# Weights decoded with their sign in the high word's Prelu, and a table that gives every operation its place

## The chip, the cores and the metric

The kernel runs on one core of a Trainium2 chip. Its engines are named as the profile names them: PE is TensorE (PE for its matmuls, PEld for its weight loads), DVE is VectorE, ACT is ScalarE, POOL is GpSimd, SP is SyncE, which issues the DMAs. The metric is the device time of one execution in microseconds (us), the median of the runs shown; lower is better.

## What is computed

The reference, cut to what matters: attention over 16 heads of 768 positions in which a key counts only if its 6-bit hash bucket is the query's, then two feed-forward blocks on 1536 tokens of 512 features.

```python
q_bits = (np.einsum('bhsd,dk->bhsk', q, proj) > 0).astype(np.int64)   # k_bits likewise
mask = q_bucket[:, :, :, None] == k_bucket[:, :, None, :]
scores = np.where(mask, scale * np.matmul(q, k.transpose(0, 1, 3, 2)), -1000000000.0)
attn = np.exp(scores - np.max(scores, axis=-1, keepdims=True))
x = np.matmul(attn / (np.sum(attn, axis=-1, keepdims=True) + 1e-09), v)
...
h = x @ w_in                                   # 512 -> 2048
x = (h * (1.0 / (1.0 + np.exp(-h)))) @ w_out   # 2048 -> 512
a, b = x @ w1, x @ w2                          # 512 -> 1024 each
out = ((a * b) @ w3) @ w_out2                  # 1024 -> 1024 -> 512
```

The weights of the feed-forward blocks reach the chip as 64-bit floating-point numbers.

## The kernel before

**Stages.** The 16 heads go by as 8 pairs of heads (n = 0 to 7), each as 12 units of 128 queries (two heads, six units each). A unit is: `scores` on PE (four matmuls into one of two score tiles), `peak` on DVE (the row maximum, L733), `exp` on ACT (L739, into one of two tiles P), `swap` on DVE (a transpose in blocks of 32, L757). When the 12 units of a pair are swapped, `weigh` on PE multiplies by V (six calls of 32 matmul statements of 32-row tiles; the profile counts two instructions for each, 64 a call), ending in four accumulators: both tiles `acc` and both tiles `turn`. `move` takes them to X, and `norm` divides by the row sums, which have gone through memory and back (`flip`, `unload`, `invert`, `send`, `spread`). Before its units, a pair needs its q and k in two parts each: `halve` (ACT or POOL), `left` (POOL, tiles qa and kb) and copies by DMA, after which `qraw` and `kraw` take the next pair's.

**Feed-forward.** w3 and the second w_out are multiplied together while attention runs (`product`, 192 matmuls of 128x512). The first block's first cells (`rise`, then `fall`, on the first 512 tokens, whose heads are done early) run there too; all other cells follow the last `weigh`. There PE has nothing but matmuls of 128x512. The tokens 512 to 1535 are multiplied in seven products of sums and differences in place of eight; their inputs (tiles y0 and y1, 14 each) are made by ACT and DVE out of X after the last pair's `norm`.

**Decoding.** All weights come in 36 pieces of two halves, 72 halves of 128x512 numbers. For each half a DMA brings 64-bit words to a tile `raw`. `high` (ACT) scales the high words into the exponent range of 32 bits, `low` (ACT or POOL) makes the top bits of the low words, `join` (DVE, L380) shifts the one and ORs the other. The sign was lost in the shift. For the 28 halves that are needed before attention ends, `high` writes to a PSUM tile (`acc`, under a token `joint`), `side` (ACT, L391) takes the sign of the high words into x, and `signed` (POOL, L394) multiplies; `raw` is given back after `side`. For the 44 others `high` writes to SBUF, and `sign` (DVE, L385) ANDs the sign bit out of `raw` and ORs it in. Then `hi` and `lo` make the two parts of a tile `piece` (lines 324, 327 and 320).

**What sets the order.** Every step is an `op` with a due time, its dependencies, the engines that it may run on with a cost in ns, and the buffers that it takes and gives. `Plan.run` plays all engines forward with these costs, picks for each engine the operation with the smallest due time among those that could start next, and emits instructions in that order; each engine then runs its own in that fixed order, with semaphores for what it needs. The due time is a formula at the place of the call, to which `shift` adds an offset from the table `OFF`, by the step's name and one of five stages. An op marked `port` is planned so that DVE and POOL don't run at the same time.

## Time and profile before

| | us |
|---|---|
| median of 3 runs (lowest to highest) | 722.84 (722.47 to 724.21) |
| span of the profiled execution | 720.6 |
| PE busy in it | 680.8 |
| DVE busy | 548.8 |
| ACT busy | 395.8 |
| POOL busy | 276.7 |

The span is from the first to the last instruction of the profiled execution; the median of the runs is 2.2 us more, which lies around the span. In the profile times are from the span's start. The last transpose of attention ends at 279.5, the last `weigh` about 293; what follows is feed-forward alone. So the question for each engine is how busy it is before 279.5, and how busy after 293. In a row of the timeline the idle time ahead of an instruction and what ended it stand in square brackets. In a row of the groups of instructions stand the count, the busy time in us, the mean of one in ns, and then the idle time ahead of them.

### The profile page before, as it was taken

What the parts mean: (1) busy time and instruction counts of PE and PEld (TensorE: products, weight loads), DVE (VectorE), ACT (ScalarE), POOL (GpSimd) and SP (SyncE); (2) the same over time, 40 slices, a digit from 0 to 9 for tenths busy, and PEclk for the clock granted to TensorE, in tenths of its full rate; (3) what the DMA queues carried; (4) which work ended last, traced back from release to release, by engine and by line L of the source; (5) the groups of instructions that cost most, each with busy time, mean ns of one, the idle gap of its engine ahead of it and who ended that gap; (6) DMA issues with size and microseconds to landing.
All of it is one profiled execution on the core that took longest, in us unless ns stands there. A gap on an engine that the chain in (4) does not pass through costs nothing.

```text
span 720.6 us, 14384 instructions
## 1 busy us (share of the span) xinstructions
PE 680.8 (94%) x5792; PEld 549.1 (76%) x5792; DVE 548.8 (76%) x799; ACT 395.8 (55%) x717; POOL 276.7 (38%) x265
## 2 busy tenths in 40 slices
PE   8697999999998999799999999999999999999997
PEld 5565777766776777688888888888888888888876
DVE  6799886958594988898889987967897637738155
ACT  5868676858585656656564453452546635323030
POOL 3967696866876711433203213022213230220000
PEclk9887899979999999999999999999999999999999
DMA  8535465655555342302212303020102220200004
GB/s 240 174 129 142 122 161 163 152 162 137 175 154 175 84 142 79 105 22 96 73 45 88 123 25 102 23 80 15 45 29 63 85 73 1 101 30 1 0 1 175
DMA packets 22883, 68.34 MB, mean 95 GB/s; under 512 B 3873, under 2 KB 4641, under 8 KB 22305
## 3 DMA queue, kind: packets, MB, share of 16 engines
q1 hardware_dynamic: 22816, 67.43, 31.0%
q8 instruction: 45, 0.74, 0.4%
q14 instruction: 22, 0.17, 0.1%
HBM read 55.58 MB, written 5.29 MB: 84 GB/s over the span
## 4 chain that ended last, share of the span: by engine, by line
PE 73%; DVE 9%; ACT 5%; issue 4%; DMA 4%; POOL 3%; SPq 0%; DVEq 0%; ACTq 0%; POOLq 0%
PE more L1181 18%; PE more L1019 14%; PE more L1137 8%; PE acc L775 7%; PE acc L1181 7%; PE score L717 5%; PE acc L1019 5%; PE turn L775 3%; PE acc L1137 2%; DVE pt L757 2%; ACT P L739 2%; PE acc L857 2%; DVE st L733 2%; DVE y L327 2%; DMA kraw<-in_kT 1%
## 5 line engine op out<-in xcount | busy, mean ns | idle before, releaser
L1019 PE MATMUL more<-y,piece 128*128 128x512 f32 x474 | 117.6, 389 | 0.7 <-ACT qraw L320 0.7
L733 DVE TENSOR_REDUCE st<-score 128x1 f32<-128x770 f32 x96 | 89.0, 941 | 33.8 <-PE score L717 31.2
L1019 PEld LDWEIGHTS more<-y,piece 128*128 128x128 f32 x474 | 88.9, 188 | 19.6 <-ACT qraw L320 1.2
L739 ACT ACTIVATE P<-score,st 128x768 f32<-128x768 f32 x96 | 85.8, 895 | 28.7 <-DVE st L733 18.4
L757 DVE STREAM_TRANSPOSE pt<-P 128x768 f32<-128x768 f32 x96 | 90.5, 958 | 5.8 <-ACT P L739 5.7
L1181 PE MATMUL more<-gh,piece 128*128 128x512 f32 x268 | 91.7, 390 | 0.1
L775 PE MATMUL turn<-pt,V 32*64 32x193 f32 x1536 | 78.4, 344 | 8.9 <-issue 8.8
L775 PE MATMUL acc<-pt,V 32*64 32x193 f32 x1536 | 77.9, 344 | 1.4 <-issue 0.8
L1200 DVE SCALAR_TENSOR_TENSOR X<-more,X 128x512 f32<-128x512 f32 x88 | 59.5, 685 | 23.7 <-PE more L1181 23.0
L775 PEld LDWEIGHTS acc<-pt,V 32*64 32x64 f32 x1536 | 60.5, 139 | 10.8 <-issue 7.5
L775 PEld LDWEIGHTS turn<-pt,V 32*64 32x64 f32 x1536 | 58.0, 138 | 12.0 <-issue 11.7
L717 PE MATMUL score<-ka,qa 128*128 128x384 f32 x168 | 51.7, 390 | 12.7 <-ACT P L739 11.3
L1137 PE MATMUL more<-x,piece 128*128 128x512 f32 x264 | 62.9, 389 | 0.0
L1181 PEld LDWEIGHTS more<-gh,piece 128*128 128x128 f32 x268 | 50.3, 188 | 10.9 <-DVE X L1200 0.5
L1137 PEld LDWEIGHTS more<-x,piece 128*128 128x128 f32 x264 | 49.6, 188 | 10.3
L717 PEld LDWEIGHTS score<-ka,qa 128*128 128x128 f32 x168 | 28.7, 201 | 33.4 <-ACT P L739 23.8
L1181 PE MATMUL more<-gl,piece 128*128 128x512 f32 x134 | 52.2, 389 | 0.0
L857 PE MATMUL acc<-piece,piece 128*128 128x512 f32 x192 | 50.3, 397 | 1.4 <-ACT X L794 1.4
L374 POOL TENSOR_SCALAR t<-raw 128x512 uint32<-128x512 uint32 x15 | 10.8, 717 | 100.9 <-DVE x L385 28.9
L370 ACT ACTIVATE t<-raw 128x512 uint32<-128x512 uint32 x46 | 30.8, 670 | 32.9 <-DMA raw<-in_w 21.1
L717 PE MATMUL score<-kb,qb 76*128 76x384 f32 x168 | 46.2, 357 | 0.6 <-DMA kb<-bits 0.6
L1181 PE MATMUL more<-piece,gh 128*128 128x512 f32 x144 | 44.3, 389 | 0.0
(195 smaller groups left out, 1450.2 us busy)
## 6 DMA issues: line engine op xcount, KB each, us to landing
raw<-in_w SPq DMA_DIRECT2D x28, 512.0 KB
raw<-in_wo SPq DMA_DIRECT2D x21, 512.0 KB
V<-in_v SPq DMA_DIRECT2D x16, 384.0 KB
raw<-in_win SPq DMA_DIRECT2D x12, 512.0 KB
qraw<-in_qT SPq DMA_DIRECT2D x8, 384.0 KB
kraw<-in_kT SPq DMA_DIRECT2D x8, 384.0 KB
invb<-inverse SPq DMA_DIRECT2D x16, 192.0 KB
out<-X SPq DMA_DIRECT2D x12, 256.0 KB
```

Of the source, the lines that this page charges most:

```text
L327: engine[e].tensor_tensor(out=dst, in0=src, in1=hi.bitcast(F32), op=ALU.subtract)
L370: nc.scalar.activation(out=plan[t], in_=pair(raw)[:, :, 0], func=AF.Copy, scale=0.875 * 2.0 ** -29, bias=0.49)
L717: nc.tensor.matmul(out=sc[:, g, :HF], lhsT=lhs[:k, qs], rhs=rhs[:k, g * HF:g * HF + HF], start=(k == 128), stop=(k != 128),)
L733: nc.vector.tensor_reduce(out=plan[uk("st")][:, 0:1], in_=plan[uk("S")][:, :, :HF + 1], op=ALU.max, axis=AX.XY, negate=True)
L739: nc.scalar.activation(out=plan[uk("P")], in_=plan[uk("S")][:, :, :HF], func=AF.Exp, bias=s[:, 0:1], accum_out=plan[key("sums")][:, par * ...
L757: nc.vector.transpose(plan[mine][:, :, 32 * i:32 * i + 32], plan[uk("P")].rearrange("p g (b i) -> p (g b) i", i=32))
L775: nc.tensor.matmul(out=to[a][64 * side:64 * side + 64, :GW + 1], lhsT=V[rows_, c, side], rhs=plan[key(f"pt{side}")][rows_, c, :GW + 1], st ...
L857: nc.tensor.matmul(out=plan[key + ("ps",)], lhsT=w[:, a, k], rhs=r[:, c], start=(k == 0 and n == 0), stop=(k == 7 and n == 2),)
L1019: nc.tensor.matmul(out=plan[bk[b]], lhsT=w[:, a], rhs=y, start=(opens and j == 0 and m == 0), stop=(j == 1 and m == 2), skip_group_check=True)
L1137: nc.tensor.matmul(out=plan[key], lhsT=w[:, a], rhs=x, start=(k == 0 and n == 0), stop=(k == 3 and n == 2))
L1181: nc.tensor.matmul(out=plan[key], lhsT=a, rhs=x, start=(f == 0 and n == 0), stop=(f == 1 and n == 2))
L1200: nc.vector.scalar_tensor_tensor(out=dst, in0=plan[key], scalar=by, in1=dst, op0=ALU.mult, op1=ALU.add)
```

## The change

**The sign.** `high` becomes Prelu, the activation that multiplies negative inputs by a slope: scale 2^-112 as before, slope -(2^32). A negative high word comes out positive with an exponent larger by 32, and the shift by 3 carries that bit into the sign bit. So `sign` (44 on DVE), `side` (28 on ACT) and `signed` (28 on POOL) are gone. All halves now go one way: `low`, then `high`, both into SBUF tiles of one pool of four x tiles (two x and two t before); `raw` is given back after both; `join` works in place. PSUM, the token `joint` and the split into early and late halves are out of it.

**The order.** `OFF`, the stages and the due times are replaced by `PLACE`: one number for each of the some 2950 operations, in the order of their creation, and the smaller goes first. Some costs of the plan are changed, and a switch of PE between `weigh` and other matmuls is given a cost of 110. Which steps exist and what each computes is otherwise the same; some buffers are given back after a few more dependencies than before. Where an engine could be chosen, a few operations change theirs.

```diff
-STAGES = (60, 210, 285, 445)
-OFF = {
...
-def shift(name, due):
-    return OFF[name][sum(due >= x for x in STAGES)] if name in OFF else 0.0
+PLACE = [
+    220, 21, 22, 23, 19, 24, 28, 29, 90, 101, 53, 93, 91, 248, 325, 328, 326, 46, 48, 50, 43, 124, 128, 210, 199, 223,
...
-PE_FREE, PE_COL, PE_TURN, PE_MORE = 13.5, 1 / 2.4, 110.0, 16.0
+PE_FREE, PE_COL, PE_TURN, PE_SWITCH = 13.5, 1 / 2.4, 110.0, 110.0
...
-        due += shift(kind or emit.__qualname__.split(".")[-1], due)
-        o = Op(on, emit, deps, due * 1000.0, take, give, size)
-        o.port = port
+        o = Op(on, emit, deps, PLACE[len(self.ops)], take, give, size)
+        o.port, o.tiled = port, tiled
...
+            if e == "PE" and o.tiled != tiled:
+                ns, tiled = ns + PE_SWITCH, o.tiled
...
-    plan.buffers("joint", [None])
...
-    plan.buffers("x", tiles(wp, "x", [128, STEP], F32, 2))
-    plan.buffers("t", tiles(wp, "t", [128, STEP], U32, 2))
+    plan.buffers("x", tiles(wp, "x", [128, STEP], F32, 4))
...
-                def high(e, raw=raw, w=w):
-                    nc.scalar.activation(out=plan[w], in_=pair(raw)[:, :, 1].bitcast(F32), func=AF.Copy, scale=2.0 ** -112)
+                def high(e, raw=raw, x=x):
+                    nc.scalar.activation(out=plan[x], in_=pair(raw)[:, :, 1].bitcast(F32), func=AF.Prelu,
+                                         scale=2.0 ** -112, alpha=-(2.0 ** 32))
...
-                def sign(e, raw=raw, x=x, m=m):
-                    engine[e].scalar_tensor_tensor(
-                        out=u32(x), in0=pair(raw)[:, :, 1], scalar=0x80000000, in1=u32(m),
-                        op0=ALU.bitwise_and, op1=ALU.bitwise_or,
-                    )
-
-                def side(e, raw=raw, x=x):
-                    nc.scalar.activation(out=plan[x], in_=pair(raw)[:, :, 1].bitcast(F32), func=AF.Sign)
-
-                def signed(e, x=x, t=t):
-                    nc.gpsimd.tensor_tensor(out=plan[x], in0=plan[t].bitcast(F32), in1=plan[x], op=ALU.mult)
-
-                a = op({"ACT": 570}, high, [load], due, [("joint", key), ("x", x), ("W", w)] if beside else [("x", x)])
-                b = op({"ACT": 570, "POOL": 590}, low, [load], due, [("t", t)])
-                j = op({"DVE": 608}, join, [a, b], due + 1, give=[w, key] if by_pool else [t] if beside else [], port=not beside)
...
+                b = op({"ACT": 570, "POOL": 590}, low, [load], due, [("x", x), ("x", t)])
+                a = op({"ACT": 570}, high, [b], due)
+                op({"": 0}, lambda e: None, [a, b], due, give=[raw])
+                j = op({"DVE": 608}, join, [a, b], due + 1, give=[t], port=True)
```

**How the order moves.** In these rows names ending in 77 and 78 are the tiles `turn`, 79 and 80 the score tiles, 81 and 82 the tiles `acc`, 83 to 89 the pieces.

PE, in the `weigh` of the fifth pair (n = 4): before, the first run of 96 `weigh` statements ends, one unit is scored, and the next run of 64 begins.

```order
L775 MATMUL turn_77<-pt_125,V_105 64x193
L717 MATMUL score_79<-ka_114,qa_110 128x384 x2
L717 MATMUL score_79<-kb_116,qb_112 128x384 x2
L775 MATMUL acc_82<-pt_127,V_105 64x193
L775 MATMUL acc_82<-pt_125,V_105 64x193
```

Now, at the same place of the same pair:

```order
L836 MATMUL turn_77<-pt_125,V_105 64x193
L777 MATMUL score_80<-ka_114,qa_110 128x384 x2
L777 MATMUL score_80<-kb_116,qb_111 128x384 x2
L777 MATMUL score_79<-ka_114,qa_110 128x384 x2
L777 MATMUL score_79<-kb_116,qb_111 128x384 x2
L836 MATMUL acc_81<-pt_127,V_105 64x193
```

Two units stand between the runs in place of one. In the fourth pair the runs were 96, 64 and 32 statements with one unit between, and are 32, 64, 64 and 32 with two; in the fifth 96, 64, 32 with one, and now with two; in the sixth 32, 64, 96 with one, and now 96, 64, 32 with two.

POOL, while the sixth pair's q and k are prepared (qa and kb by `left`, L327 before and L407 now; L394 is `signed`). Before:

```order
L327 TENSOR_TENSOR piece_88<-x_93,piece_88 128x512
L327 TENSOR_TENSOR piece_89<-x_92,piece_89 128x512
L327 TENSOR_TENSOR kb_115<-kraw_104,ka_113 64x768
L833 TENSOR_TENSOR X<-X,invb_128 128x768
L394 TENSOR_TENSOR x_93<-t_95,x_93 128x512
L324 TENSOR_SCALAR ka_114<-kraw_104 64x768
L324 TENSOR_SCALAR piece_89<-x_93 128x512
L327 TENSOR_TENSOR kb_116<-kraw_104,ka_114 64x768
L327 TENSOR_TENSOR piece_89<-x_93,piece_89 128x512
L394 TENSOR_TENSOR x_92<-t_94,x_92 128x512
L327 TENSOR_TENSOR qa_110<-qraw_103,qa_110 64x768
```

Now:

```order
L407 TENSOR_TENSOR kb_116<-kraw_104,ka_114 64x768
L407 TENSOR_TENSOR qa_110<-qraw_103,qa_110 64x768
L407 TENSOR_TENSOR piece_87<-x_93,piece_87 128x512
L451 TENSOR_SCALAR x_93<-raw_91 128x512
L894 TENSOR_TENSOR X<-X,invb_128 128x768
L681 TENSOR_SCALAR bits_108<-bits_108,sel 128x384
L407 TENSOR_TENSOR x_97<-X,x_97 128x512
L404 TENSOR_SCALAR qa_109<-qraw_103 64x768
L407 TENSOR_TENSOR kb_115<-kraw_104,ka_113 64x768
L407 TENSOR_TENSOR qa_109<-qraw_103,qa_109 64x768
```

The sign multiplications among the `left` steps (qa and kb) are gone. The steps of one head stand next to each other, the other head's after the `norm`.

PE, right behind the last `weigh`. Before, 24 matmuls of `fall` and 24 of `rise` on the first 512 tokens (x_97) come ahead of the first matmul on the others (y):

```order
L1181 MATMUL acc_81<-piece_85,piece_84 128x512 x6
L1181 MATMUL more_3493<-piece_85,piece_84 128x512 x6
L1181 MATMUL more_3494<-piece_85,piece_84 128x512 x6
L1181 MATMUL more_3495<-piece_85,piece_84 128x512 x6
L1137 MATMUL more_3496<-x_97,piece_86 128x512 x12
L1137 MATMUL more_3497<-x_97,piece_86 128x512 x12
L1137 MATMUL more_3498<-y_0_3442,piece_89 128x512
```

Now 18 come ahead of it; the 24 of `rise` stand before the last `weigh`:

```order
L1245 MATMUL acc_82<-piece_84,piece_83 128x512 x3
L1245 MATMUL acc_81<-piece_84,piece_83 128x512 x3
L1245 MATMUL acc_82<-piece_84,piece_83 128x512 x3
L1245 MATMUL more_3477<-piece_84,piece_83 128x512 x3
L1245 MATMUL more_3478<-piece_84,piece_83 128x512 x6
L1201 MATMUL more_3479<-y_0_3426,piece_88 128x512
```

Before the last `weigh` begins to run, PE has 72 matmuls of feed-forward cells behind it in the old order and 96 in the new one.

## Rows read from the trace of the kernel before

**Rows 1.** Busy time by stretch: stretch, length, each engine, granted clock, DMA.

```profile
0.00:279.50 279.50, 248.75 (x3556) 192.29 (x3556) 219.97 (x287) 195.57 (x366) 186.21 (x165) 0.93 0.53 150
293.00:720.60 427.60, 422.61 (x1854) 348.80 (x1854) 319.46 (x499) 195.40 (x343) 89.06 (x98) 1.00 0.17 57
```

**Rows 2.** The chain that ended last, in order of time: feed-forward matmuls.

```profile
587.96 14.96 PE more L1019 x66
```

**Rows 3.** Waits of DVE in 150:166, 186:200, 217:234 (total, times, longest).

```profile
DVE st L733 <- PE score L717: 8.7, 3, 5.6
...
DVE st L733 <- PE score L717: 6.9, 2, 3.7
...
DVE st L733 <- PE score L717: 5.4, 2, 5.2
DVE fv L322 <- PE turn L775: 4.5, 1, 4.5
```

**Rows 4.** Busy time by stretch, as rows 1: two of these stretches.

```profile
150.00:166.00 16.00, 15.28 (x400) 12.44 (x401) 6.69 (x10) 5.81 (x12) 7.99 (x9) 0.79 0.33 103
186.00:200.00 14.00, 12.89 (x403) 10.55 (x402) 6.16 (x10) 5.04 (x12) 10.58 (x10) 1.00 0.47 133
```

**Rows 5.** The same chain in attention: two loads and a sign step.

```profile
63.93 4.61 DMA raw<-in_w
...
95.77 3.16 DMA raw<-in_w
...
136.04 1.30 POOL x L394
```

**Rows 6.** Groups of instructions: the two DVE steps of a unit.

```profile
L757 DVE STREAM_TRANSPOSE pt<-P 128x768 f32<-128x768 f32 x96 | 90.5, 958 | 5.8 <-ACT P L739 5.7
L733 DVE TENSOR_REDUCE st<-score 128x1 f32<-128x770 f32 x96 | 89.0, 941 | 33.8 <-PE score L717 31.2 <-PE score L729 2.1
```

**Rows 7.** Timeline of PE: two units of `scores`, then `weigh`.

```profile
55.36 0.62 PE L717 MATMUL score<-ka,qa 128*128 128x384 f32 x2
...
56.97 0.39 PE L775 MATMUL acc<-pt,V 32*64 32x193 f32 x4
```

**Rows 8.** Groups of instructions: sign steps, `high`, the table load.

```profile
L394 POOL TENSOR_TENSOR x<-t,x 128x512 f32<-128x512 f32 x28 | 35.8, 1281 | 9.7 <-ACT x L391 8.1 <-POOL qa L327 1.1 <-DVE t L380 0.2
L391 ACT ACTIVATE x<-raw 128x512 f32<-128x512 f32 x28 | 18.6, 666 | 0.1
L366 ACT ACTIVATE acc<-raw 128x512 f32<-128x512 f32 x28 | 17.7, 631 | 5.0 <-PE acc L526 2.4 <-DVE t L380 2.3
L366 ACT ACTIVATE x<-raw 128x512 f32<-128x512 f32 x23 | 15.2, 668 | 7.6 <-DVE piece L327 2.6 <-DMA raw<-in_win 1.9 <-DMA raw<-in_wo 1.9
L320 ACT ACT_TABLE_LOAD x1 | 1.3, 1283 | 0.7 <-PEq L1278 0.7
```

**Rows 9.** `join`, one line's instructions (min/median/max ns): a PSUM operand, then none.

```profile
L380 DVE SCALAR_TENSOR_TENSOR t<-acc,t x28: 650/677/692, 12.3 to 235.0; 128x512 uint32<-128x512 uint32 x28
L380 DVE SCALAR_TENSOR_TENSOR t<-x,t x32: 635/684/1161, 253.2 to 636.9; 128x512 uint32<-128x512 uint32 x32
```

**Rows 10.** Groups of instructions: DVE steps that read two SBUF tiles.

```profile
L327 DVE TENSOR_TENSOR piece<-x,piece 128x512 fp32r<-128x512 f32 x38 | 28.4, 752 | 4.7 <-ACT piece L320 3.9 <-POOL piece L324 0.4
L327 DVE TENSOR_TENSOR x<-X,x 128x512 fp32r<-128x512 f32 x1 | 1.4, 1448 | 0.0
```

**Rows 11.** Groups of instructions: the eviction that frees a PSUM bank.

```profile
L1200 DVE SCALAR_TENSOR_TENSOR X<-more,X 128x512 f32<-128x512 f32 x88 | 59.5, 685 | 23.7 <-PE more L1181 23.0
```

**Rows 12.** Timeline of PE from the end of the last `weigh`.

```profile
293.42 2.93 PE L1181 MATMUL acc<-piece,piece 128*128 128x512 f32 x6 [0.45 <-ACT X L794]
...
305.87 2.88 PE L1137 MATMUL more<-y,piece 128*128 128x512 f32 x12
```

**Rows 13.** Timeline of DVE in the same stretch.

```profile
296.38 0.69 DVE L1200 SCALAR_TENSOR_TENSOR X<-acc,X 128x512 f32<-128x512 f32 x1 [1.40 <-PE acc L1181]
296.99 3.63 DVE L327 TENSOR_TENSOR y<-X,y 128x512 fp32r<-128x512 f32 x5
```

More of the change, by code (lines that the diff above doesn't have):

```diff
@@ L187, in run @@
         wire = port = 0.0
+        tiled = False
         for o in self.ops:
@@ L370, in low @@
                         nc.scalar.activation(
-                            out=plan[t], in_=pair(raw)[:, :, 0], func=AF.Copy, scale=0.875 * 2.0 ** -29, bias=0.49
+                            out=u32(t), in_=pair(raw)[:, :, 0], func=AF.Copy, scale=0.875 * 2.0 ** -29, bias=0.49
                         )
@@ L418, in piece @@
             soon, behind = need < BEGIN + SOON, need >= T_END - 20
-            h = op({"POOL": pool1(STEP), "ACT": act(STEP)} if soon or behind else {"POOL": pool1(STEP)}, hi, [j, opener], due + 3, take=first)
+            h = op({"POOL": pool1(STEP), "ACT": act_sbuf(STEP)} if soon or behind else {"POOL": pool1(STEP)}, hi, [j, opener], due + 3, take=first)
             opener = h
@@ L1097, in lsh_attention_moe_kernel @@
         users = [[], []]
+        before_that = lastly[-3:-2] if cell not in early else []
         for f in range(1 if part == 1 else 2):
@@ L1223, in lsh_attention_moe_kernel @@
         fallen.setdefault((part, c), []).extend(falls)
+        if cell not in early:
+            lastly.append(mine[bk][-1])
+        for f, last in enumerate(users):
+            risen.setdefault((part, c, f), []).extend(last)
         if kind == PAIR:
@@ L1228, in lsh_attention_moe_kernel @@
             op({"": 0}, lambda e: None, fallen[part, c], due, give=[name])
-            for of, last in zip(ofs, users):
-                op({"": 0}, lambda e: None, last, due, give=[of[0]])
+            for f, of in enumerate(ofs):
+                op({"": 0}, lambda e: None, risen[part, c, f], due, give=[of[0]])
     plan.total = plan.run()
```

144 lines of the change are left out of this document (37 added, 107 removed), and 145 rows, old and new, of the table PLACE.

## Prediction

> **What bounds the kernel now.** I read the busy time by stretch first, because a mean over the program hides that it has two parts [rows 1]. From 293 on PE is busy 422.61 of 427.60 us at full clock, with matmuls of 128x512 that follow each other every 0.227 us (66 in 14.96 [rows 2]). Nothing that another engine saves there can be seen in the time; only the number of matmuls left for this part counts, and whether PE gets new waits. Before 279.5, in attention, no engine is full: PE 248.75 of 279.5, DVE 219.97, ACT 195.57, POOL 186.21, clock 0.93. So this part is held by who waits for whom, and the waits of DVE are the next view: in three stretches, each the `weigh` of a pair, DVE stands still for 8.7, 6.9 and 5.4 us until scores come, and 4.5 until an accumulator is done: 25.5 us [rows 3]. In those stretches PE is nearly full (15.28 of 16 and 12.89 of 14), the first partly at half clock (1.2 GHz; mean 0.79) [rows 4]. PE has a long run of `weigh` there with one unit between two runs, and only two score tiles exist, so DVE runs dry. The chain that ended last, third, passes through four of the sign multiplications on POOL (1.25 to 1.30 us each, one shown) and two weight loads whose tile `raw` was given back late [rows 5].
>
> **The change, part by part.** Each term is against the profiled span of 720.6; minus is a gain.
>
> *Order at `weigh`: -9.* In the fourth to sixth pair two units stand between runs, not one: two gaps each, six units moved. A unit is a peak and a transpose on DVE, 0.941 + 0.958 = 1.90 us [rows 6], and about 0.8 on PE (two units from 55.36 to 56.97 [rows 7]). The six leave places where DVE is the busier engine, which saves 6 x 1.90 = 11.4, and go to places where PE is full, which costs 6 x 0.8 = 4.8: -6.6. The fourth pair's longest run also falls from 96 statements to 64; with some of the half-clocked time that followed I take -2.4 more. Ends: 0, if DVE's idle time only moves, and -25.5, if all of those waits go.
>
> *Sign steps of the first pair: -3.* Eight of the 28 early halves are decoded among the first 12 units. Each loses 0.666 us of ACT and 1.281 of POOL [rows 8]. Eight times 0.666 is 5.3 of ACT, which is as busy as any engine there; ends 0 and -5.3, and I take a little over half. The other 20 are counted in the next term; the 44 `sign` steps on DVE, about 0.68 each like a `join` [rows 9], lie almost all behind 279.5, under a full PE, and are worth nothing.
>
> *POOL and the loads on the chain: -4.* Four sign multiplications on the chain are 5.1 us, and POOL's order now has the `left` steps of a head side by side. `raw` no longer waits for `join` and `side`, 0.68 + 0.67, so the two loads on the chain can start some 1.35 earlier each, 2.7 together. Ends 0 and -7.8. When they go, the next late thing is the other operand of the same `scores`, so I take half.
>
> *Work moved ahead of the last transpose: +4.* By the order, DVE does five more `join`, four more `lo`, three more `gate` and one `norm` before it, and three `sign` fewer: nine steps net at 0.68 and a `norm` of about a peak's length, 0.94: +7.0. Six evictions go to ACT. Ends 0, if it falls into DVE's 59.5 idle us, and +7.0.
>
> *Feed-forward moved ahead of the last `weigh`: -5.4.* 96 matmuls in place of 72 are done by then: 24 x 0.2267. PE has 30.7 idle us in attention to hide them. Ends 0 and -5.4; I take all of it, since the second part is pure PE time.
>
> *`high` and `join` without PSUM: +2.7.* The operations stay 72 and 72, but 28 `high` write SBUF (0.668 against 0.631 [rows 8]): 1.0 us on ACT, covered by the 18.6 that `side` gives back. Prelu itself isn't in the trace. Were it half as long again as a copy, 36 in attention would add 12 us, still under that cover; below a copy's time nothing is to be had, as ACT isn't the bound. One table load stands in either program (1.283 us [rows 8]). The Trainium skill ("ScalarE: Activation LUTs", "Step-by-step: what each stage is for") says that throughput is the same for every function; no row here shows it for Prelu.
>
> All 36 `join` ahead of the last transpose now read two SBUF tiles. The 28 that had a PSUM operand never took over 692 ns; those with two SBUF operands have the same middle (684 against 677) but reach 1161 [rows 9], and other DVE steps of that kind average 752 while attention and decoding overlap, one took 1448 [rows 10]. The nearest row is 752: 36 x 0.075 = +2.7. Ends 0, at the median, and 36 x 0.771 = +27.8, if each goes like the 1448. The Trainium skill ("SBUF — State Buffer", "SBUF: two separate sides") names a reason: DVE with two SBUF inputs and GpSimd take one pair of ports in turn, each for a whole instruction; by this rule every meeting with a POOL step would cost the wait for its end, and the sum would be nearer to the upper end. It is the second rival below.
>
> *The second part: +2.* In the old order a PSUM bank is refilled 6 matmuls (1.36 us) after its last use six times, in the new one 24 times. An eviction takes 0.685 [rows 11]; with another one ahead of it on DVE the bank comes some 0.3 late. 18 x 0.3 = 5.4 is the upper end, 0 the lower; PE's order is otherwise full.
>
> *Right behind the last `weigh`: 0.* Before, 48 matmuls lie ahead of the first on y, which starts at 305.87 [rows 12], though DVE began y at 296.99 behind another eviction [rows 13]. Now 18 do. From 293.42, with the first six at half clock (2.93), they last until about 298.9, and the first y is there by 297.7; each further takes DVE 0.69 where PE uses 0.68. The cover is thin; if it is gone, up to +3. That is also the only place where the new order takes cover away from PE that I found.
>
> Sum: -9 - 3 - 4 + 4 - 5.4 + 2.7 + 2 + 0 = -12.7. Span 707.9; the median of the runs lies 2.2 above the span, so 710.1, rounded 710.
>
> **Rivals.**
>
> *The order packs better: 702.* The whole table is new, not only the places that I read. If the first term is -15 and the third -6, the sum is -20.7: 702. For: 59.5 idle us of DVE, 30.7 of PE. Against: DVE has no less work before 279.5, so most of its idle time must go at other places than the three.
>
> *`join` waits for POOL: 735, slower.* Each of 36 `join` meets a POOL step and costs 0.771 more: +27.8 in place of +2.7, 710 + 25 = 735. It decides from about 0.43 us per `join` (0.075 + 12.7/36), where the whole gain is gone. For: POOL is busy two thirds of attention, and the old code put one operand into PSUM for just these halves. Against: POOL loses 35.8 us, and the plan keeps marked steps of the two engines apart.
>
> *No change: 722.* At the three places PE is nearly full, so a unit that stands there only trades DVE's wait for PE's time, and the loads are late for other reasons. If the first three terms give a quarter, -4, the others add up to +3.3: 722.
>
> That Prelu needs its own table, with a load of 1.283 us around each, is ruled out by the order, which has one load.
>
> **How the numbers follow.** Forecast (705 to 717) 0.54, better packing 0.16, no change 0.14, waits on POOL 0.16. The predicted time is the forecast's. 700 to 725 leaves out the lower quarter of the better packing and nearly all of the last rival, not quite 0.2. Differences under 0.3%, 2.2 us, are about what a measurement of this kernel can't tell from no change. Faster by more: the first two and the edge of the third, 0.70; within it 0.13; slower 0.17.
>
> **What would show it.** Right: the last transpose ends some 8 us earlier, near 271; DVE's waits for scores in the `weigh` of the fourth to sixth pair fall by about a third; fewer half-clocked stretches; after the last `weigh` some 415 us of full PE. Wrong: `join` in attention with a mean near 1 us or more; PE waiting for DVE in the second part by more than 5 us; the same waits at other pairs; Prelu rows well over 0.67 us; idle PE between the last `weigh` and the first matmul on y.

## The result, and the profile after

The kernel after the change takes 714.57 us (median of 4 runs, 713.73 to 715.95), the kernel before 723.53 on the same chip (median of 4, 722.47 to 726.36). The ratio is 0.9877 with an interval of 0.9831 to 0.9924: faster by about 9 us. The forecast was 710, with a range of 700 to 725. Here and below a ratio and its interval leave out runs that are more than 1.5% above the fastest of their kernel, so a ratio can differ a little from that of the medians. The span of the profiled execution fell from 720.6 to 711.9, by 8.7.

Busy time by stretch of the kernel after: the stretch, its length, PE, PEld, DVE, ACT, POOL, the granted clock, the DMA share and GB/s. The first row is attention up to the last transpose, the second what follows the last `weigh`; they answer to [rows 1].

```profile
0.00:275.40 275.40, 251.03 (x3579) 198.99 (x3579) 231.37 (x287) 180.37 (x348) 159.91 (x146) 0.93 0.57 162
288.10:711.90 423.80, 418.66 (x1831) 343.95 (x1830) 295.06 (x450) 190.20 (x338) 88.91 (x96) 1.00 0.15 52
```

The last transpose ends at 275.5 in place of 279.5, so attention gave 4.0; the rest is 436.4 long in place of 441.1, so the part behind it gave 4.7. DVE is busier than before in a shorter attention (231.37 against 219.97); only three of its 44 sign steps had stood there.

The waits of DVE for scores in the `weigh` of the fourth, fifth and sixth pair, one row each, answer to [rows 3]:

```profile
DVE st L793 <- PE score L777: 2.1, 1, 2.1
...
DVE st L793 <- PE score L777: 1.0, 2, 0.6
...
DVE st L793 <- PE score L777: 4.3, 2, 3.4
```

Those stretches held 8.7, 6.9 and 5.4 us of this wait, 21.0 in all, and one of 4.5 for an accumulator; now they hold 7.4 of it. Up to the last transpose as a whole it fell from 31.2 to 20.6 (before, then after), so 3.0 of these 13.6 us came back at other places:

```profile
DVE st L733 <- PE score L717: 31.2, 19, 5.6
...
DVE st L793 <- PE score L777: 20.6, 20, 4.0
```

This is where attention gained. But it did not gain everywhere. From the ends of each pair's twelve transposes I took the time from one pair's last transpose to the next (the first number from the start; the `weigh` of the fourth, fifth and sixth pair lies in the fifth, sixth and seventh number):

| kernel | 1 | 2 | 3 | 4 | 5 | 6 | 7 | 8 | rest to the end |
|---|---|---|---|---|---|---|---|---|---|
| before | 46.2 | 28.1 | 29.8 | 32.7 | 37.6 | 34.6 | 37.2 | 33.3 | 441.1 |
| after | 44.9 | 36.9 | 29.8 | 33.9 | 30.9 | 31.7 | 32.1 | 35.3 | 436.4 |

The three of the long `weigh` runs gave 14.7 us. The second became 8.8 longer, and the fourth and eighth 3.2 together. But these intervals do not hold the same work in both kernels. The second interval by stretch, before and after, and the largest of three groups of `product` in it after:

```profile
46.20:74.30 28.10, 22.51 (x433) 17.45 (x431) 25.73 (x32) 20.25 (x39) 19.74 (x17) 0.82 0.49 132
...
44.90:81.80 36.90, 32.56 (x476) 25.45 (x469) 29.65 (x39) 22.30 (x44) 23.07 (x22) 0.82 0.53 147
...
70.46 2.90 PE L918 MATMUL acc<-piece,piece 128*128 128x512 f32 x12
```

PE is busy 10 us longer there and DVE 3.9: 24 matmuls of `product` (6.0 us) stand where there were none, and six joins where there were three. Of these 24 matmuls 19 were taken out of the third and fourth interval, which did not get shorter. In the eighth stand 24 more matmuls of `rise`. So the new order takes 15 us from one place and adds 12 at others, and a part of the 12 is work that was moved there.

The operations of the new decode, one line's instructions each (minimum, median and maximum in ns, first and last start in us), answer to [rows 8, 9]: first `join`, then `high` as Prelu.

```profile
L457 DVE SCALAR_TENSOR_TENSOR x<-x,x x60: 649/684/2302, 9.4 to 597.4; 128x512 uint32<-128x512 uint32 x60
...
L442 ACT ACTIVATE x<-raw x59: 642/664/701, 7.7 to 623.4; 128x512 f32<-128x512 f32 x59
```

Prelu takes what the copy took (664 ns in the median, and the copy to SBUF 662). `join` has the same middle as before and a maximum of 2302. Of the 36 joins ahead of the last transpose 12 are over 760 ns; together the 36 take 6.9 us more than 690 each. Each of the 12 starts while a step runs on POOL and ends some 0.55 us after that step. One of them, on DVE and then POOL:

```profile
129.93 2.09 DVE L457 SCALAR_TENSOR_TENSOR x<-x,x 128x512 uint32<-128x512 uint32 x1
...
129.67 1.81 POOL L407 TENSOR_TENSOR qa<-qraw,qa 64x768 fp32r<-64x768 f32 x1
```

In the kernel before, 22 of the 28 joins with a PSUM operand start beside a POOL step as well, and none took over 692. So the long joins are waits for POOL. The longest (2302) and one of 1303 stand side by side in the first pair. The timelines of DVE, POOL and PE there (start, length, idle time ahead in brackets):

```profile
23.85 3.53 DVE L457 SCALAR_TENSOR_TENSOR x<-x,x 128x512 uint32<-128x512 uint32 x2
27.30 1.81 DVE L793 TENSOR_REDUCE st<-score 128x1 f32<-128x770 f32 x2
...
24.68 2.15 POOL L407 TENSOR_TENSOR kb<-kraw,ka 64x768 fp32r<-64x768 f32 x1
...
30.62 0.69 PE L789 MATMUL score<-x 64*128 64x384 f32 x1 [4.33 <-ACT P L799]
```

Two joins take 3.53 us beside steps on POOL, one of which is stretched too (2.15 where its kind takes 1.83). The peaks behind them come late, then exp, and PE stands for 4.33. At the same time the granted clock falls to half for 20.5 us, from 29.3 to 49.7. The page's row of granted clock in 40 slices (tenths of full speed), of the kernel before:

```profile
PEclk9887899979999999999999999999999999999999
```

And of the kernel after:

```profile
PEclk9869699999999999999999999999999999999999
```

Before, the half-clocked stretches lie at 27 to 40, at 64 to 78, at 146 to 156 and around 250. After, they all lie ahead of 118, and the whole amount in attention is the same, 41 us in either trace.

PE from the last `weigh` on, which answers to [rows 12]:

```profile
288.69 3.90 PE L1245 MATMUL acc<-piece,piece 128*128 128x512 f32 x9 [0.47 <-ACT X L855]
...
294.48 1.52 PE L1201 MATMUL more<-y,piece 128*128 128x512 f32 x6
```

The first matmul on y follows without a wait. From 288.1 on PE is idle for 5.1 us, as before (5.0 from 292.85). Its matmuls follow each other a little less closely, though. Behind the last `weigh`, at full clock, 13 of them start more than 20 ns later than the usual 0.227 us after the one ahead, by 2.5 us together; before, 4 did, by 1.4. Three of the new places:

```profile
308.94 0.50 PE L1245 MATMUL more<-gl,piece 128*128 128x512 f32 x1 [0.37 <-DVE gl L407]
...
629.11 0.73 PE L1245 MATMUL more<-piece,gh 128*128 128x512 f32 x2 [0.16 <-DVE sg L1221]
...
630.31 0.73 PE L1245 MATMUL more<-piece,gh 128*128 128x512 f32 x2 [0.23 <-DVE sg L1098]
```

The first waits for its input, the other two for DVE steps that read their PSUM banks.

### The profile page after: what moved, and what is told of

It reads as the page before. It is cut to its first block, busy times and chain, and to the rows that moved or that the text cites. A ratio compares the mean times of both kernels' runs of the same rounds, so it can differ in the third digit from the quotient of the medians.

```text
span 711.9 us, 14222 instructions
## 1 busy us (share of the span) xinstructions
PE 679.1 (95%) x5792; PEld 551.2 (77%) x5792; DVE 531.2 (75%) x744; ACT 375.4 (53%) x694; POOL 249.5 (35%) x243
## 3 DMA queue, kind: packets, MB, share of 16 engines
q1 hardware_dynamic: 22816, 67.43, 31.7%
## 4 chain that ended last, share of the span: by engine, by line
PE 54%; DVE 4%; ACT 1%; issue 0%
PE more L1245 21%; PE more L1081 13%; PE more L1201 7%; PE acc L1081 6%; PE acc L1245 4%; PE acc L1201 3%; DVE y L407 1%; DVE gl L407 1%; DVE X L1264 1%; DVE X L1020 0%; ACT y L400 0%; DVE sg L1147 0%; ACT gh L400 0%; ACT xm L442 0%; DVE more L1098 0%
## 5 line engine op out<-in xcount | busy, mean ns | idle before, releaser
L793 DVE TENSOR_REDUCE st<-score 128x1 f32<-128x770 f32 x96 | 88.0, 946 | 24.2 <-PE score L777 20.6
L1245 PE MATMUL more<-gh,piece 128*128 128x512 f32 x312 | 105.3, 389 | 0.1
L1264 DVE SCALAR_TENSOR_TENSOR X<-more,X 128x512 f32<-128x512 f32 x101 | 68.2, 687 | 39.3 <-PE more L1245 38.7
L1081 PEld LDWEIGHTS more<-y,piece 128*128 128x128 f32 x432 | 81.1, 188 | 16.9
L1245 PEld LDWEIGHTS more<-gh,piece 128*128 128x128 f32 x312 | 58.6, 188 | 12.6 <-DVE X L1264 0.5
L457 DVE SCALAR_TENSOR_TENSOR x<-x,x 128x512 uint32<-128x512 uint32 x60 | 48.4, 810 | 17.2 <-ACT x L442 16.6
L1245 PE MATMUL more<-gl,piece 128*128 128x512 f32 x156 | 60.8, 390 | 0.4 <-DVE gl L407 0.4
L1201 PE MATMUL more<-x,piece 128*128 128x512 f32 x216 | 55.0, 389 | 0.0
L1081 PE MATMUL acc<-y,piece 128*128 128x512 f32 x198 | 52.8, 391 | 0.1
L447 ACT ACTIVATE x<-raw 128x512 uint32<-128x512 uint32 x43 | 28.9, 673 | 38.8 <-DVE piece L407 16.4
L1201 PEld LDWEIGHTS more<-x,piece 128*128 128x128 f32 x216 | 40.5, 188 | 8.4
```

The costliest lines, as they stand in the source:

```text
L447: nc.scalar.activation(out=u32(t), in_=pair(raw)[:, :, 0], func=AF.Copy, scale=0.875 * 2.0 ** -29, bias=0.49)
L457: engine[e].scalar_tensor_tensor(out=u32(x), in0=u32(x), scalar=3, in1=u32(t), op0=ALU.logical_shift_left, op1=ALU.bitwise_or)
L793: nc.vector.tensor_reduce(out=plan[uk("st")][:, 0:1], in_=plan[uk("S")][:, :, :HF + 1], op=ALU.max, axis=AX.XY, negate=True)
L1081: nc.tensor.matmul(out=plan[bk[b]], lhsT=w[:, a], rhs=y, start=(opens and j == 0 and m == 0), stop=(j == 1 and m == 2), skip_group_check=True)
L1201: nc.tensor.matmul(out=plan[key], lhsT=w[:, a], rhs=x, start=(k == 0 and n == 0), stop=(k == 3 and n == 2))
L1245: nc.tensor.matmul(out=plan[key], lhsT=a, rhs=x, start=(f == 0 and n == 0), stop=(f == 1 and n == 2))
```

## The experiments

All of these kernels but one fix the order: a list of all steps, in the order in which the changed kernel (or the kernel before) emits them, takes the place of the choice in `Plan.run`. With the list as it is, each engine's order and buffers are those of the kernel it was taken from. A row `MOVES` then moves single steps behind others, so that what is tested is that move alone. The same list is used where operations are taken out, put in or changed. A median and a ratio to the kernel before, measured on the same chip beside it, stand with each. Runs of one kernel spread by 5 to 13 us (before: 718 to 732), so 2 us are not told apart here. Each trace is of a single execution out of this spread. The list shifts the line numbers: `join` is L457 in the changed kernel and L461, L611, L613 or L614 in these.

### The decode alone

*Sign steps out, order of before.* The list of the kernel before; `high` becomes Prelu, `side`, `signed` and `sign` are empty; in the first of two kernels `high` still writes PSUM for the 28 early halves, in the second it writes SBUF. In both `raw` is still given back behind `join`.

```diff
-                    nc.scalar.activation(out=plan[w], in_=pair(raw)[:, :, 1].bitcast(F32), func=AF.Copy, scale=2.0 ** -112)
+                    nc.scalar.activation(out=plan[w], in_=pair(raw)[:, :, 1].bitcast(F32), func=AF.Prelu,
+                                         scale=2.0 ** -112, alpha=-(2.0 ** 32))
...
-                    j = op({"ACT": 570}, side, [j], due + 2, give=[raw])
-                    j = op({"POOL": pool2(STEP)}, signed, [j], due + 2.5, give=[t])
...
-                    j = op({"DVE": 608}, sign, [j], due + 2, give=[raw, t], port=True)
+                j = op({"": 0}, nothing, [j], due + 2, give=[raw] if beside else [raw, t])
+                if beside:
+                    j = op({"": 0}, nothing, [j], due + 2.5, give=[t])
```

The second kernel differs from the first in this:

```diff
-                w = key + ("w",) if beside else x
+                w = x
```

> The kernel before with each engine's order fixed as it is, and only the sign steps taken out: high is Prelu, the 28 side on ACT, the 28 signed on POOL and the 44 sign on DVE are gone; high still writes PSUM for the 28 early halves. Theory of the prediction: -3 for the sign steps of the first pair and -4 for POOL and the loads, so 716, with the loads on raw earlier. Rival, that at these places other work sets the time: 722 to 724. The 44 sign steps of DVE in the second part should give nothing by either.

> As nosign_psum, but high writes SBUF for the early halves too, so that their 28 joins read two SBUF tiles. The difference to nosign_psum is the price of these joins alone. Theory by the lengths in the changed kernel's trace (36 joins, 6.9 us over their normal length): +5 to +7 over nosign_psum, with joins of up to 2 us. The prediction's own term was +2.7. Rival, that DVE has room for them: 0 to +1.

The first took 719.00 us, ratio 0.9939 (0.9908 to 0.9971); the second 722.82, ratio 1.0010 (0.9979 to 1.0041). So the sign steps were worth 4.9, and the PSUM operand of the early joins 3.8, which is nearly all of it (by the ratios 4.4 and 5.1). That is less than the 7 and the 5 to 7 expected, by the medians, and the rivals' 0 and 0 to 1 are out. The rows of `join` show why the second is slower; those with a PSUM operand in the first kernel, then all with `raw` halves in x in the second:

```profile
L461 DVE SCALAR_TENSOR_TENSOR x<-acc,t x28: 650/678/693, 12.3 to 230.9; 128x512 uint32<-128x512 uint32 x28
```

```profile
L461 DVE SCALAR_TENSOR_TENSOR x<-x,t x60: 635/690/2398, 12.2 to 636.9; 128x512 uint32<-128x512 uint32 x60
```

None of 28 over 693 ns, against up to 2398: in attention 15 of 31 are over 760 in the second kernel, 11.4 us over 690 each, and all 15 start beside a POOL step. The last transpose ends at 272.7 in the first and 278.2 in the second. From the last `weigh` to the end they take 427.5 and 427.7, as before (427.7): the `sign` steps of DVE there were worth nothing.

*The decode with the old due times.* The new decode block in the kernel before, where `OFF` and `Plan.run` order it anew.

```diff
-                a = op({"ACT": 570}, high, [load], due, [("joint", key), ("x", x), ("W", w)] if beside else [("x", x)])
+                a = op({"ACT": 570}, high, [load], due, [("x", x)])
                 b = op({"ACT": 570, "POOL": 590}, low, [load], due, [("t", t)])
-                j = op({"DVE": 608}, join, [a, b], due + 1, give=[w, key] if by_pool else [t] if beside else [], port=not beside)
...
+                op({"": 0}, lambda e: None, [a, b], due, give=[raw])
+                j = op({"DVE": 608}, join, [a, b], due + 1, give=[t], port=True)
```

> The kernel before, its due times and its table OFF unchanged, with the new decode alone (Prelu, no sign steps, joins of two SBUF tiles). Theory that the order made the gain: the decode alone is worth what its own terms were in the prediction, -3 for the sign steps of the first pair, -4 for POOL and the loads on the chain, and for the joins +7 rather than +2.7, because the 36 joins of attention averaged 874 ns in the changed kernel where 28 with a PSUM operand averaged 671: together about 0, so 722 to 723. Rival, that the decode made it: 715 to 718, with the DVE waits for scores at weigh in the fourth to sixth pair much as before.

733.73 us, ratio 1.0129 (1.0083 to 1.0176): slower by 10, where nearly the same decode in the order of before is even. Both theories missed it. The two differ in when `raw` is given back (here after `high` and `low`), in order and in the choice of engines, and by 9 to 11 us. So the table `OFF`, made for one set of steps, gave a worse order for another, even a smaller one.

*The sign steps put back into the new order.* Early halves only, right behind their `join`; no other step moves.

```diff
+                if beside:
+                    aside = op({"ACT": 570}, side, [j], behind=j)
+                    free.deps.append(aside)
+                    j = op({"POOL": pool2(STEP)}, signed, [aside], give=[t], behind=aside)
```

> The changed kernel with each engine's order fixed as it is, and the 28 early halves' sign steps put back right behind their join (side on ACT, 0.67 us each, then a multiplication on POOL, 1.28 each; raw given back after side). No other instruction moves. Theory of the prediction: sign steps and late loads were worth 3 and 4, so 714.6 + 7 = about 721.5. Rival, that ACT and POOL had the time and the loads were not what held attention: within 2 of 714.6.

745.62 us, ratio 1.0304 (1.0267 to 1.0341), 31 above the changed kernel, where 7 was expected. Two rows of its waits ahead of 290 (total, times, longest):

```profile
ACT x L619 <- DVE x L613: 25.1, 23, 4.8
...
PE score L944 <- ACT P L966: 23.6, 17, 4.7
```

`side` (L619) comes to its place on ACT before its `join` (L613) is done, 23 times, and the `exp` steps behind it wait, and PE for them. ACT's waits for weights grew too, since `raw` is given back later, but less: from 7.8 to 12.3 us. So this is no price of the sign steps as such: for the most part it is what dependent steps cost in a fixed order that has no gap left for them. The first kernel above gives the fair price, 4.9.

### The order at `weigh`

*One unit between runs, as before, in the new order.*

```diff
+MOVES = ((477, 406), (473, 410), (490, 412), (482, 490), (486, 482), (494, 486), (581, 514), (586, 516), (590, 586), (694, 618), (702, 620), (698, 702))
```

Each pair of numbers is a `scores` step and the `weigh` or `scores` step that it now follows.

> The changed kernel with each engine's order fixed, but in the fourth to sixth pair one unit of scores stands between two runs of weigh, with runs of 96, 64 and 32 as before the change, and the units taken out follow the last run. Theory of the prediction: the first term is undone, +9 (bounds 0 and 25), so 722 to 725, and DVE's waits for scores there are 5 us or longer each again. Rival, that a unit there only trades DVE's wait for PE's time: 714 to 716.

735.07 us, ratio 1.0134 (1.0086 to 1.0183), 20 above the changed kernel. DVE's waits for scores in the three `weigh` are back, though only one of them is over 5 us, as was expected of each:

```profile
DVE st L947 <- PE score L931: 7.6, 1, 7.6
...
DVE st L947 <- PE score L931: 4.6, 2, 4.4
...
DVE st L947 <- PE score L931: 4.2, 2, 3.1
```

The fifth to seventh interval take 39.8, 36.8 and 33.5 us, 15.4 more than in the changed kernel, and run 13.6 us at half clock, where the changed kernel has none; another 3.1 lie in the first interval, where the order is the same, with a half-clocked stretch from 15.2 to 22.0 that the changed kernel's trace has not. So the rival is out and the first theory holds in direction; its 722 to 725 was too little. The 20 are no clean price of the term either: four units now stand in a row behind the last run of the fourth and fifth pair, which was not so in the kernel before.

*Two units in a gap, in the order of before.*

```diff
+MOVES = ((494, 490), (495, 491), (496, 492), (497, 493), (498, 410), (502, 498), (598, 594), (599, 595), (600, 596), (601, 597), (602, 514), (606, 602), (694, 614), (698, 694), (699, 695), (700, 696), (701, 697), (702, 618), (706, 702))
```

> The kernel before with each engine's order fixed, old decode and all, and only units of scores moved: in the fourth and fifth pair both units that stood in two gaps stand in the first (runs of 96 and 96), in the sixth the runs are 96, 64 and 32 with two units and one. Theory, that two units in a gap keep DVE fed during a long run: a part of the first term (-9 forecast; 14.8 us shorter in the fourth interval between last transposes to the seventh by the trace), -4 to -9, so 714 to 719, and DVE's waits of 5 us for scores gone. Rival, that the gain needs the rest of the new order: within 2 of 723.

728.21 us, ratio 1.0056 (1.0029 to 1.0083): slower by 4, not faster. In the fourth and fifth pair this made runs of 96 and 96 statements with two units between, not the three to four runs of the new order. Waits of DVE in the three `weigh`:

```profile
DVE fv L402 <- PE turn L855: 3.8, 1, 3.8
...
DVE fv L402 <- PE turn L855: 6.5, 1, 6.5
...
DVE fv L402 <- PE turn L855: 5.1, 1, 5.1
```

The waits for scores shrank (3.2, 2.9, 3.7), but now DVE stands at `move`, which needs the end of the `weigh`. Neither the theory (-4 to -9) nor its rival (no change) came true. In the new order ACT has more of the moves: 20 of its steps ahead of the last transpose are such, 14 before, and DVE has 8 in place of 14. So two units in a gap are not worth 15 by themselves. Which part of the rest of the new order makes them pay, these moves, the shorter runs or other steps on DVE, no run here separates.

### Feed-forward ahead of the last `weigh`

The 24 matmuls of the third `rise` cell go behind the last `weigh`.

```diff
+MOVES = ((1726, 828), (1727, 1726), (1728, 1727), (1729, 1728), (1730, 1729), (1731, 1730), (1732, 1731), (1733, 1732))
```

> The changed kernel with each engine's order fixed, and the 24 matmuls of the third rise cell, which ran before the last weigh, put behind it. Theory of the prediction: they were free in attention and cost their own time behind it, 24 x 0.2267 = 5.4, so 720. Rival, that in attention they cost about as much as behind it: 714 to 716.

726.44 us where 720 was expected, ratio 1.0055 (1.0022 to 1.0088), 12 above the changed kernel in the median; its profiled execution is 7.9 longer: 9.5 behind the last `weigh`, which itself ends 1.6 earlier. The stretch from the last `weigh` on, and three rows of PE's timeline in it:

```profile
286.50:719.80 433.30, 425.46 (x1858) 348.03 (x1854) 297.42 (x453) 191.26 (x340) 88.34 (x96) 1.00 0.16 52
```

```profile
287.08 7.27 PE L1355 MATMUL acc<-x,piece 128*128 128x512 f32 x24 [0.45 <-ACT X L1009]
...
295.76 1.66 PE L1399 MATMUL acc<-piece,piece 128*128 128x512 f32 x6 [0.73 <-DVE kraw L1301]
...
306.81 3.47 PE L1355 MATMUL more<-y,piece 128*128 128x512 f32 x14 [1.50 <-DVE y L561]
```

PE is busy 6.8 us longer there (the 24 take 7.27, in part at half clock), and idle 2.7 longer, since the gate of the moved cell and then y come late. In attention the matmuls were not quite free: the eighth interval, where they stood, is 33.1 without them and 34.7 to 36.2 in the eight traces that have them there. So they cost some 2 us of their 5.4 ahead of the last `weigh`, and more than 5.4 behind it.

### What the new order lost

*Joins of the first pair behind the peaks.* In the first version the two joins alone are moved, in the second the steps on ACT and DVE that need them too.

```diff
+MOVES = ((887, 81), (873, 887))
```

> The changed kernel with each engine's order fixed, and only two joins of the first pair moved: at 23.85 us they took 3.53 us together where two take 1.36, beside multiplications on POOL, and the two peaks behind them came late; here they stand behind those two peaks. Theory, that waits of joins for POOL cost time and started the half-clocked stretch of 29 to 49.5: PE's idle 4.33 us ahead of 30.6 falls to 2 or less, the stretch gets shorter, and the time is 708 to 712. Rival, that this wait has slack and the clock falls anyway: 714 to 715.

```diff
+MOVES = ((887, 81), (873, 887), (888, 82), (874, 888), (875, 83), (889, 875))
```

> As in joins_later, the two joins of the first pair behind the two peaks, and now what hangs on them too: the two steps on ACT that make the high part stand behind the two exps, the two on DVE that make the low part behind the next swaps. In joins_later ACT still stood 3.65 us for the joins ahead of the exps. Theory: the exps start near 26.8 in place of 29.6, PE's idle 4.33 us falls to about 1.5, and the time by 2 to 4, to 711 or 712. Rival, that the first pair is held at half clock anyway: 714 to 715.

The first took 715.85 us, ratio 0.9893 (0.9851 to 0.9934); ACT still stood 3.65 for the joins, and PE 4.49. The second took 713.07, ratio 0.9871 (0.9832 to 0.9910). The runs tell neither from the changed kernel. PE and DVE of the second:

```profile
27.62 0.44 PE L943 MATMUL score<-x 64*128 64x384 f32 x1 [0.68 <-ACT P L953]
...
35.49 0.68 PE L943 MATMUL score<-x 64*128 64x384 f32 x1 [3.98 <-ACT P L953]
```

```profile
27.27 2.55 DVE L611 SCALAR_TENSOR_TENSOR x<-x,x 128x512 uint32<-128x512 uint32 x2
```

PE's wait at this place fell from 4.33 to 0.68, as expected, and stands one pair of units later, with 3.98; the two joins met POOL at their new place as well (2.55 where two take 1.36). The wait was moved, not removed.

*Two `scores` steps in the order of their peaks.* In the changed kernel PE scores one unit of the second pair at 54.18, while DVE stands at the peak of the other one, which is scored later: 3.97 us idle ahead of 59.85.

```diff
+MOVES = ((157, 94), (161, 96))
```

> The changed kernel with each engine's order fixed, and two scores steps of the second pair exchanged on PE, so that they come in the order in which DVE's peaks take them. In the changed kernel PE scored the later one first, at 54.18, while DVE stood at the other's peak until 59.85 (3.97 us idle). Theory, that this inversion is a part of what the second pair lost (36.9 us against 28.1 before): DVE's wait there falls under 1 us and the time by 3 to 4, to 711. Rival, that the units behind are late anyway (ACT, POOL, half clock): 714 to 715.

714.23 us, ratio 0.9892 (0.9855 to 0.9929): no difference to the changed kernel. DVE at this place:

```profile
56.24 1.75 DVE L611 SCALAR_TENSOR_TENSOR x<-x,x 128x512 uint32<-128x512 uint32 x1
57.92 1.81 DVE L947 TENSOR_REDUCE st<-score 128x1 f32<-128x770 f32 x2
```

The wait is gone. Counted from the last transpose of the first pair, the peak comes 3.8 earlier (11.1 after it in place of 14.9), although a join ahead of it now meets POOL (1.75). The second interval fell to 33.0; but in four kernels that leave these two steps alone it is 32.6 to 34.5 as well, and the fourth was 38.8 in this execution. So no gain of this exchange is shown, and what the second and fourth interval lost is not settled by these runs.

*`join` with one operand.* The OR of the low word is left out.

```diff
-                    engine[e].scalar_tensor_tensor(
-                        out=u32(x), in0=u32(x), scalar=3, in1=u32(t), op0=ALU.logical_shift_left, op1=ALU.bitwise_or
+                    engine[e].tensor_scalar(
+                        out=u32(x), in0=u32(x), scalar1=3, scalar2=None, op0=ALU.logical_shift_left
```

> The changed kernel with each engine's order fixed, and join as a shift of its first operand alone: the OR of the low word is left out, so DVE reads one SBUF tile and not two. Theory, that a join with two SBUF operands waits for POOL: none takes over 0.8 us (twelve of 36 in attention did, up to 2.30), and the 6.9 us over their normal length in attention go; with what a shorter instruction saves beyond that (unknown, at most 0.35 each), the time falls by 3 to 12, to 703 to 712. Rival, that the long ones have another cause: some stay over 0.9 us.

717.59 us, ratio 0.9888 (0.9853 to 0.9923): no gain, though the step itself is 260 ns shorter.

```profile
L611 DVE TENSOR_SCALAR x<-x x67: 383/425/2030, 9.5 to 631.1; 128x512 uint32<-128x512 uint32 x67
```

It still takes up to 2030 ns; 11 of the 36 in attention are over 500, all of which start beside a POOL step, and the 36 take 7.6 us over 425 each, no less than the joins' 6.9. So the theory failed and the rival's sign, some over 0.9, came true, though the cause is still POOL: a step need not have a second SBUF operand to wait for POOL; this one has a single operand, and is faster than any join (425 against 684). Why the shorter step gave no time is open. The Trainium skill ("SBUF — State Buffer", "SBUF: two separate sides") names two kinds of DVE step that lock the shared ports: those with two SBUF inputs, and those in a performance mode that uses two ports. The row is in line with the second kind; that this step runs in such a mode no run here shows.

*Seven of the twelve long joins with a PSUM operand, in the new order.* Only those for which an accumulator is free at their place, so that no step moves.

```diff
-                b = op({"ACT": 570, "POOL": 590}, low, [load], due, [("x", x), ("x", t)])
-                a = op({"ACT": 570}, high, [b], due)
...
+                beside, w = (serial[0], n) in ((3, 0), (4, 0), (3, 512), (7, 0), (8, 0), (9, 512), (15, 512)), key + ("w",)
+                h = w if beside else x
...
+                a = op({"ACT": 570}, high, [b], due, [("W", w)] if beside else [])
```

> The changed kernel with each engine's order fixed, and for seven of the twelve joins that were long in attention high writes a free accumulator in PSUM, as the old decode did, so that the join reads one SBUF tile; no instruction changes its place. In the changed kernel's trace these seven took 3.9 us over the normal length together. Theory, that waits for POOL at joins are a loss the change still carries: the seven fall under 0.70 us each and the time by 2 to 4, to 711 to 713. Rival, that POOL makes other DVE steps or later joins wait in their place, or that attention is held elsewhere: 714 to 716.

711.27 us, ratio 0.9826 (0.9762 to 0.9889): the fastest median of all, 3.3 under the changed kernel's, and faster than before by its interval; the intervals of the two overlap, so that it beats the changed kernel is likely and not shown. The joins with a PSUM operand:

```profile
L614 DVE SCALAR_TENSOR_TENSOR x<-acc,x x7: 646/669/684, 25.7 to 232.2; 128x512 uint32<-128x512 uint32 x7
```

All seven are under 0.70, as the theory had it, and no other join took up their wait: those in attention are 3.8 us over 690 each, down from 6.9.

## Why the prediction was right, point by point

The time fell by 9 where 13 was forecast. Ahead of the last transpose it fell by 4.0, where the terms add up to 9.3, and behind it by 4.7, where they add up to 3.4. The largest gain and the price of the joins were sized too small, two other gains too large, and longer intervals at other pairs were not foreseen; that the sum came within 4.6 is in part luck.

- **Order at `weigh`, -9: right in direction, its reason incomplete.** The three intervals around it gave 14.7, and 15.4 went when one unit was put between runs again. Of the 14.7 a part is clock: before, 11.1 us there ran at half clock, after, none. The kernel without sign steps in the order of before, with 0.3 us at half clock there, takes 105.0 for the three, the changed kernel 94.7: 10.3, near the term. DVE's waits for scores fell by about two thirds, not by one. But two units in a gap, put alone into the order of before, made it slower, so the units are not the whole reason.
- **Sign steps, -3, and POOL and loads, -4: right in direction, a little too large.** Together 4.9 by the runs in the order of before (2.1 to 6.7 by the interval of the ratio). The two are not told apart, and that loads came earlier is not shown: ACT's waits for weights ahead of the last transpose are 13.9 us before and 14.8 without the sign steps; they are 7.8 in the changed kernel. That `sign` on DVE was worth nothing under a full PE is shown (427.5 against 427.7).
- **`join` without PSUM, +2.7: right mechanism, sized too small.** 3.8 in the order of before. By length the joins of the changed kernel are 6.9 over their normal time, 0.19 each, not 0.075. The row taken as nearest (752 ns) was misread: it is a mean over the program, and 30 of its 38 steps lie behind the last transpose. The 8 ahead of it average 810, which would have given 36 x 0.133 = 4.8:

```profile
L327 DVE TENSOR_TENSOR piece<-x,piece 128x512 fp32r<-128x512 f32 x8 | 6.4, 810 | 2.5 <-ACT piece L320 2.0 <-POOL piece L324 0.4
```

- **The rival built on this, 0.77 each, was far too harsh.** One in three met POOL, not all. The plan keeps these joins apart from POOL, and POOL has less to do (159.91 against 186.21); in the order of before, whose plan did not keep 28 of them apart, it was 15 of 31.
- **Work ahead of the last transpose, +4.** DVE is busy 11.4 longer there; 6.9 are the long joins, about 1 are peaks and transposes that are each 4 to 5 ns longer, and the rest, some 3.5, is this term, less the six moves that went to ACT. Whether it lies on the path was not tried by itself.
- **Feed-forward moved ahead, -5.4: right in direction, too large.** From the last `weigh` on the time fell by 4.0 (427.7 to 423.7), and some 2 us were paid for it in the eighth interval. Putting the matmuls back cost 9.5 behind the last `weigh`, more than their own time, because the gate and y then came late. Behind the last `weigh` PE is busy 418.7 us where the prediction put some 415 (by its own figures 422.6 - 5.4 = 417.2).
- **Second part, +2: near in size, for the most part by another cause.** 24 matmuls fewer are 5.4 us, and the part behind the last `weigh` is 4.0 shorter; late starts of PE account for some 1.2 of the difference (2.5 against 1.4). Waits for a bank, as the prediction argued, are 1.7 of the 2.5 and all of the 1.4, so they grew by 0.3; the rest is the late input at 308.94 and smaller delays.
- **Right behind the last `weigh`, 0, and Prelu: right.** The 18 matmuls last 5.8 us (the prediction's own figures give 5.65, and so 299.1 in place of its 298.9), and y is there.
- **The last transpose at 271: missed by 4.5.** The half-clocked stretches are fewer, four in place of six, but as long in all, 41 us. The step that failed is not a term of the sum but the silence about the first four pairs and the last: I compared the orders at three places where before waits, and gave the new order no losses elsewhere but one. The second interval is 32.6 to 37.3 in seven traces that keep the new order there, against 27.9 to 30.4 in the four that keep the old one; the fourth 33.9 to 40.7 against 32.0 to 33.2. In the second, more work stands now. The fourth has no half-clocked time in the four traces with the old order and 3.4 to 13.7 us in eight with the new one (`scores_swapped` among them), and the two with 13.7 are the longest (38.8 and 40.7). Whether the clock makes these intervals long, or the waits in them the clock, stays open; moving single waits away did not bring them back.

In sum: the decode by itself, in the order of before, is worth nothing that the runs can tell (722.82 against 723.85; ratio 1.0010, 0.9979 to 1.0041), because its joins give back most of what the sign steps were. So the gain is the order's, together with the buffers that came with it; this is worked out as a difference, for the new order was not tried with the old decode. The rival "no change" is thus true of the decode, and "better packing" of the places in the middle of attention.

## What to carry to other kernels

When an operation is taken out, look at where its operands now lie: here a PSUM operand had kept 28 steps clear of another engine, and losing it cost nearly what the removed operations were worth. A whole new order should be compared at all stages, by the time from one landmark to the next, and not only where the old one waits: here it took 15 us from one place and added 12 at others. With the times, count the work in each interval, or moved work looks like a loss. And a table of due times or places belongs to its set of steps: with steps added or taken out it is no longer the same order's price that one measures, unless the order is held fixed.

## What the runs showed of the hardware

- A DVE step with two SBUF operands that starts while POOL works can wait for the end of POOL's step: all 12 joins over 760 ns in the changed kernel's attention, and all 15 in the kernel without sign steps, started beside one. With a PSUM operand none waited (63 joins in three traces, at most 693 ns), though 22 of the 28 in the kernel before started beside a POOL step.
- A DVE step with one SBUF operand that takes 425 ns meets POOL in the same way, up to 2030 ns.
- POOL loses at such a meeting too: a multiplication of 64x768 that began during a join took 2.15 us where its kind takes 1.83.
- The granted clock in attention falls to half for 31 to 68 us in all, in pieces of 3 to 20 us, and the pieces differ between executions whose order is the same up to there: the trace of `scores_swapped` has one from 13.7 to 20.6, ahead of its first moved step, where the changed kernel's has none. Longer runs of a kernel mostly have the lower mean clock; those of `join_one` go from 709 us at a mean clock of 0.973 to 719 at 0.954.
